# Filling a 0/1 attention mask by row-copying DMAs between SBUF partitions, in a fused attention and FFN kernel

## The chip, the cores and the metric

The kernel runs on one core of a Trainium2 chip. The metric is the device time of one execution, in microseconds (us). The engines are named as in the profile: PE is TensorE (PEld its weight loads), DVE is VectorE, ACT is ScalarE, POOL is GpSimd and SP is SyncE. "PEq", "SPq" and so on are their instruction queues.

## The reference

Block-sparse attention (batch 4, 8 heads, 768 positions, head size 64, blocks of 32) feeds a gated feed-forward network (FFN). Shortened:

```python
scores = q @ k.T / 8
mask = window of +-1 block | first/last block row and column | 3 random blocks per block row
attn = softmax(where(mask, scores, -1e9))
x = (attn @ v), heads side by side           # 3072 x 512
out = (sigmoid(x @ w_gate) * (x @ w_val)) @ w_out   # 512 -> 1536 -> 512, f32
```

The mask has 24 x 24 blocks. It is the same for all batches and heads, and depends on an input (`sampled_blocks`), so the kernel has to make it.

## The kernel before

Keys lie on partitions, queries along the free axis. Partition p of key tile t holds token 6p + t. So partition 16a + i of tile t belongs to block row 3a + (6i + t)//32. The tile `mask` is 128 partitions x 6 key tiles x 768 queries of f16. The 24 block rows, widened to 768 columns, are in `mb24` (24 partitions). A matmul with a 24 x 128 selector spreads them over the partitions, and DVE copies the result from PSUM:

```python
def mask_tile(c0, c1, t):
    n = c1 - c0
    w = 512 // n
    bank = Bank("m")
    def mm(eng):
        for i in range(w):
            nc.tensor.matmul(spare[bank.slot][:, i * n : (i + 1) * n],
                e24[:, (t + i) * 128 : (t + i + 1) * 128], mb24[:, c0:c1],
                start=True, stop=True)
    def evac(eng):
        copy(eng, mask[:, t : t + w, c0:c1],
             spare[bank.slot].rearrange("a (w n) -> a w n", w=w))
    a = plan.add([(PE, 0.25)], mm, t_rows, at=12.0, take=[bank])
    return plan.add([(DVE, 0.69)], evac, [a], free=[bank])
# ...
# Step.mul: exp(scores) times the mask, for all query units but the first
m = mask[:, 2 * self.j : 2 * self.j + 2, self.u * UQ : (self.u + 1) * UQ]
nc.vector.tensor_tensor(self.pt, self.pt,
    m.unsqueeze(1).broadcast_to([128, 2, 2, UQ]), op=ALU.mult)
```

Work is cut into 12 units of 256 queries (4 batches x 3). The first unit adds a bias by matmul and needs no mask; unit 1 is the first to multiply by it. The FFN of unit n runs beside the attention of unit n + 1. `plan.add(engines, fn, deps)` gives tasks with estimated costs to a planner, which fixes each engine's instruction order when the kernel is built. On the chip every engine kept that order, and waited where its next instruction was not ready (in the changed kernel DVE stood for 14.76 us at one instruction, and ran the one behind it, which did not need what was waited for, only then). With a list of two engines the planner takes the one that is free first.

Inputs are f32 and are cast to f16 by the loads, which GpSimd issues. The order is q, k, v of batch 0 in pieces, the first quarter of the FFN weights, the rest of q of batch 0 (the "late q load"), the other FFN weights, and then k, q, v of batch 1. The last three are issued only once the copies of batch 0 have freed the buffers and GpSimd's earlier issues, some of which wait for the landing of older loads (in the kernel before, the issue at 17.48 us after a wait of 1.05 us), are through.

The softmax here doesn't subtract the row's maximum and nothing guards it: scores larger than these inputs give would overflow.

Of the kernel before, what the change touches and what calls it, by code (L numbers as in the profile page):

```python
# [20 lines left out]
B, H, S, D = 4, 8, 768, 64  # L21
BLK = 32
NB = S // BLK
NT = S // 128
# [6 lines left out]
UQ = 256  # L31
NU = S // UQ
PE, ACT, DVE, DMA = "PE", "ACT", "DVE", "DMA"
# [90 lines left out]
def kernel(  # L124
# [11 lines left out]
    nc = tc.nc  # L136
# [34 lines left out]
    e24 = e64[0:NB, :]  # L171
    bias = sing.tile([128, UQ], f16)
    mask = sing.tile([128, NT, S], f16)
# [54 lines left out]
    mb24 = sing.tile([NB, S], f16)  # L228

    def copy(eng, dst, src):  # L230
        if eng == ACT:
            nc.scalar.copy(dst, src)  # L232
        else:
            nc.vector.tensor_copy(dst, src)  # L234
# [22 lines left out]
    plan = Plan({'m': 4, 's': 2})  # L257
    spare = [ps.tile([128, 512], f32, name=f"m{i}") for i in range(4)]
# [5 lines left out]
    def ring(nm, bufs):  # L264

        i = len(used[nm]) - bufs
        return [used[nm][i]] if i >= 0 else []

    def m16(slot):
        return spare[slot].bitcast(f16)  # L270
# [25 lines left out]
    t_rows = []  # L296
    bank = Bank("m")
# [19 lines left out]
    mm = plan.add([(PE, 0.25)], bias_mm, [t_mb], take=[bank])  # L317
    plan.add([(PE, 0.9)], lambda eng: warm(2), [mm])
    t_bias = plan.add([(DVE, 0.35)], bias_out, [mm])
    t_rows.append(plan.add([(DVE, 0.6), (ACT, 0.6)], rows_out, [t_bias], at=12.0, free=[bank]))  # L320

    def more_rows():
        bank = Bank("m")

        def more_mm(eng):
            nc.tensor.matmul(
                spare[bank.slot][0:NB, 0 : S - 512],
                mb16[:, 0:NB],
                e24[:, 512:S],
                start=True,  # L330
                stop=True,
            )

        def more_out(eng):
            copy(eng, mb24[:, 512:S], spare[bank.slot][0:NB, 0 : S - 512])

        mm = plan.add([(PE, 0.15)], more_mm, [t_mb], at=12.0, take=[bank])
        t_rows.append(plan.add([(DVE, 0.35), (ACT, 0.37)], more_out, [mm], free=[bank]))

    def mask_tile(c0, c1, t):  # L340
        n = c1 - c0
        w = 512 // n
        bank = Bank("m")

        def mm(eng):
            for i in range(w):
                nc.tensor.matmul(  # L347
                    spare[bank.slot][:, i * n : (i + 1) * n],
                    e24[:, (t + i) * 128 : (t + i + 1) * 128],
                    mb24[:, c0:c1],  # L350
                    start=True,
                    stop=True,
                )

        def evac(eng):
            copy(
                eng,
                mask[:, t : t + w, c0:c1],
                spare[bank.slot].rearrange("a (w n) -> a w n", w=w),
            )  # L360

        a = plan.add([(PE, 0.25)], mm, t_rows, at=12.0, take=[bank])
        return plan.add([(DVE, 0.69)], evac, [a], free=[bank])

    def prep(src, dst, b, p, t0, t1, deps, at):

        bank = Bank("m")
        box = []

        def pair(eng):  # L370
            pr = work.tile([128, NT, 2, D], f16, tag="pr", bufs=PB, name="pr")
            box.append(pr)
            nc.vector.tensor_copy(  # L373
                pr[:, t0:t1, :, :],
                src[:, 2 * p : 2 * p + 2, t0:t1, :].rearrange(
                    "a h t d -> a t h d"
                ),
            )

        def turn(eng):  # L380
            for t in range(t0, t1):
                nc.tensor.transpose(  # L382
                    m16(bank.slot)[:, (t - t0) * 128 : (t - t0 + 1) * 128],
                    box[0][:, t, :, :],
                    ident,
                )

        def evac(eng):
            copy(
                eng,  # L390
                dst[b % 2][:, p, t0 * 128 : t1 * 128],
                m16(bank.slot)[:, 0 : (t1 - t0) * 128],
            )

        n = t1 - t0
        a = plan.add([(DVE, 0.15 + 0.035 * n)], pair, ring("pr", PB) + loaded[b], at=at)
        copies[b].append(a)
        c = plan.add([(PE, 0.058 * n)], turn, [a], take=[bank])
        used["pr"].append(c)
        return plan.add(  # L400
            [(DVE, 0.14 + 0.07 * n), (ACT, 0.18 + 0.1 * n)], evac, [c] + deps, free=[bank]
        )

    def pair_up(src, dst, b, p, deps, at):
# [77 lines left out]
    class Pair:  # L482
# [72 lines left out]
        def xt(self):  # L555
            if self.n >= 2:
                deps = [used["xT"][self.n - XB]] if self.n >= XB else []
                c = plan.add([(DMA, 0.05)], self.xbar, [self.normed] + deps, lag=6.0)
                used["x16"].append(c)
                xdone[self.n].append(c)  # L560
                return
            c = plan.add([(PE, 0.12)], self.turn, [self.normed], take=[self.bank2])
            used["x16"].append(c)
            deps = [used["xT"][self.n - XB]] if self.n >= XB else []
            xdone[self.n].append(
                plan.add([(DVE, 0.29), (ACT, 0.37)], self.evac, [c] + deps,
                         free=[self.bank2])
            )

# [153 lines left out]
    masks, kdone, qdone, vdone, read, turned_b = {}, {}, {}, {}, {}, {}  # L723
    preps, valued, turned = deque(), deque(), deque()

    def prep_k(b, p, at=0.0):
        kdone[b, p] = [prep(k16, kT, b, p, 0, NT, [], at)]

    def prep_q(b, p, at=0.0, t0=0, t1=NT):
        d_ = [prep(q16, qT, b, p, t0, t1, [], at)]  # L730
        for u in range(t0 // 2, t1 // 2):
            qdone[b, p, u] = d_
# [87 lines left out]
    for p in range(NP):  # L820
        prep_q(0, p, land["q2", None], 2, NT)
    more_rows()
    for t in range(0, NT, 2):
        m = [mask_tile(UQ, S, t + i) for i in range(2)]
        for u in (1, 2):
            masks[t // 2, u] = m
    for j in range(3):
        preps.append(lambda j=j: masks.update({(j, 0): [mask_tile(0, UQ, 2 * j)]}))
    later(1)

    parts = deque()
# [5 lines left out]
    for n in range(1, len(units)):  # L837
        b, u = units[n]
# [63 lines left out]
```

## Time and profile before

| | before |
|---|---|
| time, 3 runs | 298.45 us median (298.33 to 299.55) |
| span of the profiled run | 297.6 us |
| PE busy | 289.9 us (97%) |
| first mask multiply starts | 27.10 us |
| FFN of unit 0 starts on PE | 29.3 us |
| casting loads end (packet records) | about 53 us |

These lines are from the page of the kernel before. The slices cut the span into 40 equal parts of 7.4 us; a digit is the busy share in tenths (PEclk: the granted clock in tenths of full speed; DMA: the mean of 16 engines). GB/s is what the DMA engines moved. Then come the chain of work that ended last, as shares of the span, and one group of instructions: after its count stand the busy time in us and the mean ns of one.

```profile
PE 289.9 (97%) x3302; PEld 206.2 (69%) x3302; DVE 191.0 (64%) x439; ACT 205.1 (69%) x323; POOL 48.5 (16%) x65
...
PE   7998999999999999999999999999999999999994
...
PEclk9999999999999999999999999999999999999999
DMA  7999999999900200999940202920201200201101
GB/s 109 185 201 203 206 204 205 212 174 149 193 12 9 90 13 10 173 177 133 179 70 18 83 11 56 203 64 20 79 11 20 79 11 20 78 15 20 70 2 71
...
PE 92%; ACT 2%; DMA 2%; DVE 1%; POOL 1%; issue 0%; ACTq 0%; POOLq 0%
...
L234 DVE CAST mask<-m 128x512 f16<-128x512 f32 x9 | 5.7, 681 | 0.4 <-PE m L347 0.4
```

PE is the limit. The DMA engines are full from the second slice to the eleventh; up to about 53 us that is the casting loads, at about 200 GB/s. The nine mask copies cost 5.7 us of DVE, and DVE has 36% of the span free.

The chain of the kernel before, around the place where the mask is first used (start us, duration us, what):

```profile
26.14 2.77 ACT pt L469 x3
...
28.95 0.39 PE s L459 x4
29.34 0.98 PE m L617 x8
```

The same stretch in the timeline of the kernel before (start us, duration us, engine, line, operation, tiles, and in brackets the idle time before and what ended it):

```profile
26.61 0.88 POOL L188 DMA_DIRECT2D k<-in_k_dram  x1 [1.45 <-DVE mask L234]
...
27.10 0.69 DVE L475 TENSOR_TENSOR pt<-pt,mask 128x1024 f16<-128x1024 f16 x1 [0.18 <-ACT pt L469]
...
29.28 0.39 PE L617 MATMUL m<-xT,wg 128*128 128x256 f16 x2
```

The first mask multiply starts at 27.10 us, 0.18 us after the DVE instruction before it, and it waited for the exp on ACT, not for the mask. So the mask costs nothing in waiting here. FFN tile 0 (L617) follows at 29.3.

### The profile page before, as it was taken

The numbers are of one execution on the slowest core, as the hardware profiler recorded it, in microseconds if no ns is written. First come the engines' busy times: TensorE is split into PE (matmuls) and PEld (weight loads), VectorE is DVE, ScalarE is ACT, GpSimd is POOL, SyncE is SP. The second block draws the span as 40 slices with busy tenths as digits, with TensorE's granted clock in tenths as the row PEclk, the third lists the DMA queues.
The fourth block names the chain that finished last, engine by engine and source line by source line (L and its number), as shares of the span: only waits on it lengthen the run. The fifth ranks groups of instructions, "written<-read, shape, count | busy, mean of one in ns | idle before, by whom it ended". The sixth has DMA issues, their size and how long they took to land.

```text
span 297.6 us, 7862 instructions
## 1 busy us (share of the span) xinstructions
PE 289.9 (97%) x3302; PEld 206.2 (69%) x3302; DVE 191.0 (64%) x439; ACT 205.1 (69%) x323; POOL 48.5 (16%) x65
## 2 busy tenths in 40 slices
PE   7998999999999999999999999999999999999994
PEld 2655785786786786786776786686687687687771
DVE  3588877875675677676576577577477477475240
ACT  2689977677677677677777776777777677672331
POOL 8944100197000000097100000000000000000000
PEclk9999999999999999999999999999999999999999
DMA  7999999999900200999940202920201200201101
GB/s 109 185 201 203 206 204 205 212 174 149 193 12 9 90 13 10 173 177 133 179 70 18 83 11 56 203 64 20 79 11 20 79 11 20 78 15 20 70 2 71
DMA packets 74540, 28.55 MB, mean 96 GB/s; under 512 B 57352, under 2 KB 71560, under 8 KB 74504
## 3 DMA queue, kind: packets, MB, share of 16 engines
q0 software_dynamic: 40400, 14.16, 43.7%
q1 hardware_dynamic: 33924, 13.75, 20.5%
q8 instruction: 26, 0.43, 0.6%
q10 hardware_dynamic: 180, 0.13, 0.1%
q14 instruction: 10, 0.08, 0.1%
HBM read 28.55 MB, written 6.29 MB: 117 GB/s over the span
## 4 chain that ended last, share of the span: by engine, by line
PE 92%; ACT 2%; DMA 2%; DVE 1%; POOL 1%; issue 0%; ACTq 0%; POOLq 0%
PE m L617 44%; PE m L657 22%; PE s L459 12%; PE m L497 12%; DMA k<-in_k_dram 2%; ACT pt L469 2%; PE s L451 1%; PE m L382 1%; PE m L347 1%; ACT qT L232 0%; PE m L518 0%; POOL k L188 0%; ACT kT L232 0%; POOL q L188 0%; POOL v L188 0%
## 5 line engine op out<-in xcount | busy, mean ns | idle before, releaser
L469 ACT ACTIVATE pt<-s 128x1024 f16<-128x1024 f32 x144 | 139.9, 1023 | 9.5 <-PE s L459 9.4
L475 DVE TENSOR_TENSOR pt<-pt,mask 128x1024 f16<-128x1024 f16 x132 | 91.0, 690 | 52.0 <-ACT pt L469 51.9
L628 ACT ACTIVATE th<-m 128x256 f32<-128x256 f32 x144 | 54.3, 388 | 48.0 <-PE m L617 47.2
L617 PE MATMUL m<-xT,wg 128*128 128x256 f16 x576 | 86.8, 273 | 0.3 <-DVE x L509 0.3
L617 PE MATMUL m<-xT,wv 128*128 128x256 f16 x576 | 86.4, 273 | 0.0
L633 DVE SCALAR_TENSOR_TENSOR ht<-th,m 128x256 f16<-128x256 f32 x144 | 56.6, 417 | 20.8 <-ACT th L628 20.5
L657 PE MATMUL m<-wo,ht 128*128 128x512 f16 x288 | 66.1, 380 | 0.0
L617 PEld LDWEIGHTS <-wv 128*128 128x128 f16 x576 | 56.3, 98 | 6.5
L617 PEld LDWEIGHTS <-wg 128*128 128x128 f16 x576 | 50.5, 98 | 14.8 <-issue 9.7
L657 PEld LDWEIGHTS <-ht 128*128 128x128 f16 x288 | 26.5, 98 | 32.8 <-issue 4.2
L459 PE MATMUL s<-qT,kT 64*128 64x256 f16 x576 | 48.0, 275 | 1.1 <-ACT pt L469 0.8
L497 PEld LDWEIGHTS <-pt 128*128 128x128 f16 x1152 | 43.3, 98 | 3.8 <-issue 0.6
L497 PE MATMUL m<-vex,pt 128*128 128x65 f16 x1152 | 45.1, 194 | 0.0
L459 PEld LDWEIGHTS <-kT 64*128 64x128 f16 x576 | 23.0, 95 | 17.4 <-issue 13.6
L694 ACT ACTIVATE ysb<-m 128x512 f32<-128x512 f32 x23 | 13.7, 597 | 23.7 <-PE m L657 23.7
L740 POOL DMA_DIRECT2D kp<-in_k_dram x16 | 13.0, 820 | 80.8 <-DMA kT<-kp 53.7
L509 DVE TENSOR_TENSOR x<-m,rz 128x256 f16<-128x256 f32 x48 | 20.4, 424 | 1.7
L507 DVE RECIPROCAL rz<-m 128x4 f32<-128x4 f32 x48 | 8.7, 181 | 15.1 <-PE m L497 15.1
L740 POOL DMA_DIRECT2D qp<-in_q_dram x16 | 13.0, 819 | 2.2 <-DMA kp<-in_k_dram 1.9
L451 PE MATMUL s<-bias,e 64*128 64x256 f16 x48 | 7.2, 319 | 0.2 <-ACT pt L469 0.2
L382 PE MATMUL m<-ident,pr 128*128 128x128 f16 x48 | 5.2, 264 | 0.8 <-DVE pr L373 0.4
L234 DVE CAST mask<-m 128x512 f16<-128x512 f32 x9 | 5.7, 681 | 0.4 <-PE m L347 0.4
(45 smaller groups left out, 67.2 us busy)
## 6 DMA issues: line engine op xcount, KB each, us to landing
out_dram<-ysb SPq DMA_DIRECT2D x23, 256.0 KB, 2.0
v<-in_v_dram POOLq DMA_DIRECT2D x3, 768.0 KB, 11.1
wg<-in_moe_w_gate_dram POOLq DMA_DIRECT2D x4, 384.0 KB, 12.8
wv<-in_moe_w_val_dram POOLq DMA_DIRECT2D x4, 384.0 KB, 14.0
wo<-in_moe_w_out_dram POOLq DMA_DIRECT2D x3, 512.0 KB, 16.9
kp<-in_k_dram POOLq DMA_DIRECT2D x16, 96.0 KB, 5.8
qp<-in_q_dram POOLq DMA_DIRECT2D x16, 96.0 KB, 4.9
k<-in_k_dram POOLq DMA_DIRECT2D x4, 192.0 KB, 5.8
```

What stands on the lines that cost most here:

```text
L451: nc.tensor.matmul(score[self.bank.slot][:, o // D, i, :], e64[o : o + D, t * 128 : (t + 1) * 128], bias[o : o + D, :], start=True, stop=F ...
L459: nc.tensor.matmul(score[self.bank.slot][:, o // D, i, :], kT[b % 2][o : o + D, p, t * 128 : (t + 1) * 128], qT[b % 2][o : o + D, p, u * U ...
L469: nc.scalar.activation(self.pt, score[self.bank.slot], AF.Exp, bias=0.0, scale=SCALE)
L475: nc.vector.tensor_tensor(self.pt, self.pt, m.unsqueeze(1).broadcast_to([128, 2, 2, UQ]), op=ALU.mult,)
L497: nc.tensor.matmul(self.acc[:, s, a, :], self.steps[t // 2].pt[:, a, t % 2, s * 128 : (s + 1) * 128], vex[self.b % 2][:, 2 * self.p + a, t ...
L509: nc.vector.tensor_tensor(self.x16, self.acc[:, :, :, 0:D], rz.broadcast_to([128, 2, 2, D]), op=ALU.mult,)
L617: nc.tensor.matmul(pg[:, i, :], w[:, c, f * 128 : (f + 1) * 128], xTs[self.n][0][:, c, :], start=(c == 0), stop=(c == 3),)
L628: nc.scalar.activation(th, spare[bank.slot][:, 0:UQ], AF.Tanh, bias=0.0, scale=0.5)
L633: nc.vector.scalar_tensor_tensor(self.ht[:, f, :], in0=box[0], scalar=1.0, in1=spare[bank.slot][:, UQ : 2 * UQ], op0=ALU.add, op1=ALU.mult,)
L657: nc.tensor.matmul(spare[bank.slot], self.ht[:, f, s * 128 : (s + 1) * 128], wo[:, f, :], start=(f == 0), stop=(f == NF - 1),)
L694: nc.scalar.activation(ysb, spare[bank.slot], AF.Copy, bias=0.0, scale=0.5)
L740: nc.gpsimd.dma_start(dst[:, p, :, a, :], src[b, 2 * p + a].rearrange("(n t) d -> n t d", t=NT),)
```

## The change

The intent is to take the mask off PE and DVE. After `mb24` is ready, 18 DMAs on SP copy its rows to the partitions of `mask`. Each DMA serves 8 partitions, 16 apart, which take 8 different rows, and repeats each row for up to six key tiles: 8 x 6 pieces of 1536 B. In all that is 768 pieces and 1.18 MB. Beside it, the head's copies out of PSUM that ACT could also take are given to DVE alone (except one).

```diff
-    t_rows.append(plan.add([(DVE, 0.6), (ACT, 0.6)], rows_out, [t_bias], at=12.0, free=[bank]))
+    t_rows.append(plan.add([(DVE, 0.6)], rows_out, [t_bias], at=12.0, free=[bank]))
-    def mask_tile(c0, c1, t):           # (body cut)
+    def mask_rows(deps):
+        parts = ((0, 0, 5, 0, 6), (0, 5, 6, 0, 2), (1, 5, 6, 2, 6), (1, 6, 10, 0, 6),
+                 (1, 10, 11, 0, 4), (2, 10, 11, 4, 6), (2, 11, 16, 0, 6))
+        def go(eng):
+            rows = mb24.rearrange("(a c) n -> a c n", c=3)
+            dst = mask.rearrange("(a i) t n -> a i t n", i=16)
+            for c, i0, i1, t0, t1 in parts:
+                for i in range(i0, i1):
+                    nc.sync.dma_start(dst[:, i, t0:t1, :],
+                        rows[:, c, :].unsqueeze(1).broadcast_to([8, t1 - t0, S]))
+        return plan.add([(DMA, 0.05)], go, deps, lag=8.0)
...    # prep(): copies of qT and kT
-            [(DVE, 0.14 + 0.07 * n), (ACT, 0.18 + 0.1 * n)], evac, [c] + deps, free=[bank]
+            [(DVE, ...), (ACT, ...)][: 2 - ((b, p) != (0, 0))], evac, [c] + deps, free=[bank]
...    # copies of xT, units 0 and 1
-                plan.add([(DVE, 0.29), (ACT, 0.37)], self.evac, [c] + deps,
+                plan.add([(DVE, 0.29)], self.evac, [c] + deps,
...    # every mask (j, u) now depends on the one task mask_rows(t_rows)
```

The planner is told `lag=8.0`: it orders the engines as if the mask landed 8 us after its issue. In the order that it then fixes, DVE has the first mask multiply ahead of the last xT copy of unit 0 and of all FFN gating.

More of the change, by code (lines that the diff above doesn't have):

```diff
@@ L338, in more_rows @@
         t_rows.append(plan.add([(DVE, 0.35), (ACT, 0.37)], more_out, [mm], free=[bank]))
-    def mask_tile(c0, c1, t):
-        n = c1 - c0
-        w = 512 // n
-        bank = Bank("m")
-        def mm(eng):
-            for i in range(w):
-                nc.tensor.matmul(
-                    spare[bank.slot][:, i * n : (i + 1) * n],
-                    e24[:, (t + i) * 128 : (t + i + 1) * 128],
-                    mb24[:, c0:c1],
-                    start=True,
-                    stop=True,
-                )
-        def evac(eng):
-            copy(
-                eng,
-                mask[:, t : t + w, c0:c1],
-                spare[bank.slot].rearrange("a (w n) -> a w n", w=w),
-            )
-        a = plan.add([(PE, 0.25)], mm, t_rows, at=12.0, take=[bank])
-        return plan.add([(DVE, 0.69)], evac, [a], free=[bank])
+    def mask_rows(deps):
+        parts = (
+            (0, 0, 5, 0, 6),
+            (0, 5, 6, 0, 2),
+            (1, 5, 6, 2, 6),
+            (1, 6, 10, 0, 6),
+            (1, 10, 11, 0, 4),
+            (2, 10, 11, 4, 6),
+            (2, 11, 16, 0, 6),
+        )
+        def go(eng):
[3 more added lines that the diff above has]
+                for i in range(i0, i1):
+                    nc.sync.dma_start(
+                        dst[:, i, t0:t1, :],
+                        rows[:, c, :]
+                        .unsqueeze(1)
+                        .broadcast_to([8, t1 - t0, S]),
+                    )
+        return plan.add([(DMA, 0.05)], go, deps, lag=8.0)
     def prep(src, dst, b, p, t0, t1, deps, at):
@@ L400, in prep @@
         return plan.add(
-            [(DVE, 0.14 + 0.07 * n), (ACT, 0.18 + 0.1 * n)], evac, [c] + deps, free=[bank]
+            [(DVE, 0.14 + 0.07 * n), (ACT, 0.18 + 0.1 * n)][: 2 - ((b, p) != (0, 0))], evac, [c] + deps, free=[bank]
         )
@@ L822 @@
     more_rows()
-    for t in range(0, NT, 2):
-        m = [mask_tile(UQ, S, t + i) for i in range(2)]
-        for u in (1, 2):
-            masks[t // 2, u] = m
+    rows = [mask_rows(t_rows)]
     for j in range(3):
-        preps.append(lambda j=j: masks.update({(j, 0): [mask_tile(0, UQ, 2 * j)]}))
+        for u in range(NU):
+            masks[j, u] = rows
     later(1)
```

## The prediction

> **What bounds it now.** TensorE: the page gives PE 289.9 of 297.6 us busy (97%), the chain of waits 92% PE. From about 36 us the timeline shows matmuls back to back. Slack exists only before: the chain has ACT pieces at 16.0 (0.80 us), 25.0 (1.10), 26.1 (2.77, exps) and 33.3 (1.03), then DVE until 35.95.
>
> **Removed.** 12 mask matmuls: 1.5 us of PE chain (1.9% of its first 80 us). Nine mask copies on DVE, 5.7 us busy. Moved from ACT to DVE: the 24x512 row copy (0.56), one kT copy (0.80), two qT copies (0.58 each), late xT copies (0.37 each): about 3.5 us of ACT where ACT is in the chain. Alone this is worth 2 to 3.5 us.
>
> **Added.** 18 DMAs on the SP queue, 768 row pieces of 1536 B, 1.18 MB. As built, the first VectorE mask multiply waits for nearly all of them; behind it stand the last xT copy and all FFN gating, so TensorE must stop before FFN tile 0 (29.3 us now). The first DMA can go when the second row copy ends, about 16.8 us.
>
> The slices show the DMA engines at 9 of 9 and about 205 GB/s from 10 to 53 us: the casting loads. [...]here 8, so 96 pieces each. [...]at 77 to 79 us, beside a load, about 7 store packets per 0.1 us started over 16 engines, and 16 load packets: one store packet per engine each 0.23 us. For the smaller 1536 B pieces (65 ns each in the e64 load) I estimate 0.12 to 0.2 us, so 11 to 19 us for 96. With 1.4 us of start-up the mask lands at 29 to 38 us, middle 33.5.
>
> The loads lose that time on the same engines: the late q load, landed at about 22.3 us, comes 2 to 4 us later, and with it unit 1's scores, so FFN tile 0 starts no earlier than about 31 us. Later loads mostly still make their use.
>
> **Sum.** FFN tile 0 starts at mask + 1.1 us (multiply, xT copy), about 34.6, 5.3 later than now. One score step more is left by then, +0.4; the ACT gap at 33 to 36 us is filled, -1.5; a long stall may return the PE clock to its slow start rate (0.21 instead of 0.11 us per matmul before 14 us), +0.5. That makes 303; weighing a quicker mask, 302 us, range 296 to 309. Faster by over 2%: 0.04; within: 0.61; slower: 0.35.
>
> **What would show it.** Mask issues from about 17 us; the first multiply waiting on DMA, at 29 to 38 us instead of 27.1; TensorE idle just before FFN tile 0; the chain through mask DMAs; then dense matmuls, same tail. ACT busy lower by 3.5 us, DVE by 3.
>
> **What would make it wrong.** If the pieces spread over 16 engines[...], the mask lands by 26 us: a gain of 2 to 3 us. If [...]issue is slow (over 0.8 us per DMA), it lands after 40 us: 309 or more.

Marked cuts take out the general grounds that were given for two figures, and two cases that rested on them; no trace of this case shows them as rules. No term of the sum is cut. The mask: issue at 16.8 us, 1.4 of start-up and 15.3 for 96 pieces (the middle of 11 to 19) make 33.5. The time: 5.3 us by which FFN tile 0 is later, + 0.4 - 1.5 + 0.5, make 4.7 us more than before, 303 us, weighed down to 302. "Here 8" is the number of DMA engines to one mask DMA: it was an assumption then, and the records of the changed kernel, below, agree with it (eight landing increments for each). The 1.4 us is an estimate for which no source was given: in the kernel before, SP's stores had their first packet 0.83 to 0.84 us after the start of the issue where the queue was quiet. That a stall may slow the PE clock was a guess as well; the rates beside it, 0.21 and 0.11 us, are of the kernel before, and the clock after the stall was measured below.

## The result, and the profile after

The changed kernel takes 313.64 us (median of 4 runs, 313.1 to 314.1) against 298.89 (median of 4 on the same chip). The ratio is 1.0492, 95% interval 1.0459 to 1.0524. Ratios are the mean time of one kernel's fast runs over that of the other's of the same rounds, so they are not quite the ratio of the medians quoted. The prediction of 302 us (296 to 309) was too low.

| | before | after |
|---|---|---|
| span of the profiled run | 297.6 | 311.6 |
| mean granted PE clock | 0.998 | 0.973 |
| mask usable | not waited for | 40.9 us |
| first mask multiply | 27.10 | 41.17 |
| FFN tile 0, as in the chain | 29.34 | 42.12 |
| from there to the end | 268.3 | 269.5 |

The page after, the lines that answer to those above. Slices are of 7.8 us. The last line is a group of DMA issues (count, KB each) and stands in the place of the mask copies, which are gone:

```profile
PE 286.9 (92%) x3290; PEld 204.6 (66%) x3290; DVE 188.3 (60%) x438; ACT 202.1 (65%) x315; POOL 48.6 (16%) x65
...
PE   6874059999999999999999999999999999999995
...
PEclk9799559999999999999999999999999999999999
DMA  7999999669993020089992020193110110110101
GB/s 114 181 210 193 194 201 193 103 138 189 133 182 71 19 73 16 17 154 178 144 214 19 8 86 12 41 175 92 44 53 8 44 53 8 44 54 18 69 0 67
...
PE 85%; DMA 9%; DVE 2%; POOL 1%; issue 1%; ACT 0%; DVEq 0%; SPq 0%; POOLq 0%
...
mask<-mb SPq DMA_DIRECT2D x14, 72.0 KB
```

PE is idle in the fifth slice (31 to 39 us), and its clock is halved there and in the next. In the eighth slice (55 to 62 us) the DMA engines move only 103 GB/s; what this is, the packet records below show. The chain of waits after, where it passes through the mask:

```profile
17.86 0.14 SPq L358
...
18.04 6.37 DMA mask<-mb
...
24.43 8.09 DMA mask<-mb
...
32.53 8.33 DMA mask<-mb
...
41.17 0.13 DVE pt L477
...
41.78 0.30 DVE xT L234
...
42.12 1.23 PE m L619 x5
```

Three DMA flights in a row make up the stall. At most eight of the 18 DMAs are out at a time: in the program as built, the ninth waits for the landing of the first, the seventeenth for the ninth. So three flights of 6.4, 8.1 and 8.3 us follow one another. Then the multiply, the xT copy behind it in DVE's order, and FFN tile 0. The timeline after shows the same from the side of DVE and PE:

```profile
41.17 0.69 DVE L477 TENSOR_TENSOR pt<-pt,mask 128x1024 f16<-128x1024 f16 x1 [14.76 <-DMA mask<-mb]
...
41.78 0.28 DVE L234 COPY xT<-m 128x256 f16<-128x256 f16 x1
...
42.12 0.37 PE L619 MATMUL m<-xT,wg 128*128 128x256 f16 x1 [14.23 <-DVE xT L234]
```

DVE waited 14.76 us for the mask, and PE 14.23 us for an xT copy that does not need the mask at all but stands behind the multiply.

The shift of FFN tile 0, 42.12 - 29.34 = 12.8 us, is most of the loss. Is the work behind it the same? The windows from FFN tile 0 to the end say so. The columns are the window's length, then busy us (and count) of PE, PEld, DVE, ACT and POOL, the granted clock, the DMA share and GB/s. Before:

```profile
29.34:297.60 268.26, 264.12 (x3013) 191.14 (x3012) 171.51 (x384) 185.38 (x300) 29.03 (x36) 1.00 0.59 87
```

After:

```profile
42.12:311.60 269.48, 265.77 (x3013) 191.13 (x3012) 172.79 (x388) 184.03 (x296) 28.12 (x35) 0.99 0.55 82
```

The same 3013 matmuls took 1.65 us more of PE time, and the idle time among them fell from 4.1 to 3.7 us (length less busy time). Five-microsecond windows of the kernel after show where the slow matmuls are:

```profile
30.00:35.00 5.00, 0.00 (x0) 0.00 (x0) 0.00 (x0) 0.00 (x0) 0.88 (x1) 0.66 1.39 194
35.00:40.00 5.00, 0.00 (x0) 0.00 (x0) 0.00 (x0) 0.00 (x0) 0.87 (x1) 0.50 1.34 189
40.00:45.00 5.00, 2.88 (x15) 1.54 (x15) 2.69 (x5) 1.01 (x2) 0.87 (x1) 0.50 1.31 203
45.00:50.00 5.00, 5.00 (x70) 3.20 (x69) 3.89 (x9) 3.99 (x8) 0.00 (x0) 0.97 1.28 205
```

From 30 to 40 us PE, DVE and ACT do nothing, while the DMA engines move 190 GB/s. The clock records of the trace have it at half from 31.7 to 45.3 us. PE has been idle since 27.9 us when the clock falls 3.8 us later, and it is full again 3.2 us after PE restarts at 42.12.

The trace also records every DMA packet: start, queue, size, duration. Counted in stretches of 3 us, they are not a view of the page but a sum over the records:

```
stretch us   before: loads KB/us   after: loads KB/us   after: mask KB/us (pieces)
24 to 27            199                  130                  63  (123)
30 to 33            201                  130                  63  (123)
45 to 48            199                  202                   0
54 to 57              0                  109                   0
57 to 60              0                  102                   0
```

While the mask pieces run, the total is as before (193 against 200 KB/us), so every mask byte is taken from the loads. After the loads of before are over, those of after go on at half rate until 64.7 us. That is what is left if eight of the 16 engines fell behind and the other eight are done. The semaphore records of the trace fit: after one increment at its issue, each mask DMA lands by eight more, and of the 16 with which k of batch 1 lands, eight came at 45.4 to 47.6 us and eight at 55.5 to 57.3 (in the kernel before, all between 43.7 and 45.6). From the eight increments and the half rate I take it that each mask DMA used eight engines. (Experiment 5 has DMAs of the same shape alone on the engines: there the mean busy share of the 16 was three to four tenths.) I work out an estimate from the table and these eight: if the eight engines without mask pieces kept their half of 200 KB/us, the other eight carried about 30 KB/us of loads, or about 118 load packets of 768 B in 3 us beside 123 mask pieces. So there is about one load packet to each mask piece. And 123 pieces on eight engines in 3 us is one per engine each 0.195 us.

The first piece starts at 21.4 us, 4.2 us after the first issue at 17.2. The last starts at 39.6.

### The profile page after: what moved, and what is told of

Its sections match the earlier page's. It is cut to its first block, busy times and chain, and to the rows that moved or that the text cites. A ratio compares the mean times of both kernels' runs of the same rounds, so it can differ in the third digit from the quotient of the medians.

```text
span 311.6 us, 7854 instructions
## 1 busy us (share of the span) xinstructions
PE 286.9 (92%) x3290; PEld 204.6 (66%) x3290; DVE 188.3 (60%) x438; ACT 202.1 (65%) x315; POOL 48.6 (16%) x65
## 4 chain that ended last, share of the span: by engine, by line
PE 85%; DMA 9%; DVE 2%; POOL 1%; issue 1%; ACT 0%; DVEq 0%; SPq 0%; POOLq 0%
PE m L619 42%; PE m L659 21%; PE s L461 11%; PE m L499 11%; DMA mask<-mb 7%; DMA k<-in_k_dram 2%; POOL k L188 0%; POOL q L188 0%; POOL v L188 0%; DVE kT L234 0%; DVE vex L430 0%; DVE mb L234 0%; DVE pr L375 0%; PE m L384 0%; PE m L520 0%
## 5 line engine op out<-in xcount | busy, mean ns | idle before, releaser
L619 PEld LDWEIGHTS <-wv 128*128 128x128 f16 x576 | 56.7, 98 | 21.3 <-issue 14.4
L384 PE MATMUL m<-ident,pr 128*128 128x128 f16 x48 | 4.1, 235 | 3.6 <-DVE pr L375 3.6
L453 PE MATMUL s<-bias,e 64*128 64x256 f16 x48 | 6.5, 296 | 0.3 <-ACT pt L471 0.3
L384 PEld LDWEIGHTS <-pr 128*128 128x128 f16 x48 | 3.0, 104 | 5.2 <-DVE pr L375 5.0
```

The lines of the kernel that those rows point to most:

```text
L619: nc.tensor.matmul(pg[:, i, :], w[:, c, f * 128 : (f + 1) * 128], xTs[self.n][0][:, c, :], start=(c == 0), stop=(c == 3),)
```

## The experiments

The main theory: the mask lands late because its 768 pieces share eight DMA engines with the casting loads, and the DVE multiply waits for it with the xT copy behind. The rivals, taken up in turn: the head copies moved from ACT to DVE; the added traffic by itself, without any wait; a fixed time per piece, whatever its size; the partitions that a DMA writes or reads; and the DMAs' issue on SP.

### 1. The head copies alone

The kernel before, with only the moves from ACT to DVE:

```diff
-[(DVE, 0.6), (ACT, 0.6)], rows_out
+[(DVE, 0.6)], rows_out
 # and the same for the copies of kT and qT (but one) and of xT
```

> The mask stays with matmuls and copies as before; only the head copies are moved to VectorE. Theory (the loss is the wait for the mask DMAs): 297.5 to 300 us, ratio 0.997 to 1.006, because TensorE is dense from 36 us on and the moved copies only trade ACT slack for VectorE work in a stretch where VectorE still has 5.7 us of mask copies. Rival (the moved copies delay VectorE and make part of the 15 us): over 302 us.

Measured: 300.62 us (299.44 to 301.08), ratio 1.0065, interval 1.0042 to 1.0089. This is about 2 us of loss and just outside the top of the range expected. It is not the cause of 15 us, but the prediction's "alone this is worth 2 to 3.5 us" does not hold: the moves gave nothing by themselves. I have not tested why they cost 0.65%. That stays open.

### 2. The DMAs alone

The changed kernel with the head copies put back as before.

```diff
-[(DVE, 0.6)], rows_out
+[(DVE, 0.6), (ACT, 0.6)], rows_out
 # and the same for kT, qT and xT
```

> The mask comes by the 18 DMAs; the head copies may go to ACT as before. Theory (the mask DMAs are the whole loss): the last mask DMA lands at 40 to 41 us as in the changed kernel, and the time is 311 to 315 us. Rival (copies on VectorE hold up the rows that feed the DMAs and are part of the loss): 310 us or less.

Measured: 314.27 us (313.37 to 315.05), ratio 1.0528, interval 1.0504 to 1.0552. DVE waited 14.4 us for the mask, as its waits between 14 and 75 us show (total us, times, longest):

```profile
DVE pt L477 <- DMA mask<-mb: 14.4, 1, 14.4
```

All of the loss comes with the DMAs.

### 3. The traffic without the wait

The kernel before, with its matmul-made mask and its order on PE, DVE and ACT, and in addition the 18 DMAs into a tile that nobody reads:

```diff
+    mask2 = sing.tile([128, NT, S], f16, name="mask2")
+    # mask_rows as in the change, but dst = mask2.rearrange(...)
+    mask_rows(t_rows)
     for t in range(0, NT, 2):
         m = [mask_tile(UQ, S, t + i) for i in range(2)]
```

> Kernel before with the same compute order, plus the 18 mask DMAs into a tile that nobody reads. It separates the cost of the traffic from the cost of the wait. Theory: the loads lose engine time on the eight engines that the mask uses and end at about 63 us instead of 53; the batch 1 k load, used at 47.0 us, lands at 52 to 57, so VectorE stops at the kp copies and the kernel takes 301 to 307 us. Rival (only the wait costs): 298.3 to 299.5 us.

Measured: 309.37 us (308.72 to 309.58), ratio 1.0361, interval 1.0343 to 1.038. This is well above the range expected, and the theory as I held it (that nearly everything is the mask wait) falls. Without one instruction waiting for the mask DMAs, they cost 10.8 us. The chain of this kernel shows through what:

```profile
32.80 23.99 DMA k<-in_k_dram
56.81 1.17 DVE kp L436 x4
57.98 0.34 DVE ht L661
```

And its waits between 14 and 75 us (engine, line, what it waited for: total us, times, longest):

```profile
DVE kp L436 <- DMA k<-in_k_dram: 8.1, 1, 8.1
...
PEld L685 <- DVE ht L661: 5.1, 1, 5.1
```

k of batch 1 was issued at 32.80, not at 26.61. (The trace puts GpSimd's wait before it down to a DVE instruction that ended at 32.55. In the changed kernel the same issue comes at 32.59, after a wait of 4.66 us that is put down to the landing of a weight load. I take the late loads for the cause in both, but no run separates the two.) It then shared the engines with what was left of the others, and landed at 56.8 (45.6 in the kernel before). DVE stands still for it at the `kp` copies, which repack k, and with it the FFN gating (`ht`) that PE needs. The granted clock was halved in the eighth slice, at 54 to 62 us.

### 4. Half the bytes

Key tiles 2j and 2j + 1 of one partition always lie in the same block row, so half a mask is enough. This is the changed kernel with 18 DMAs that repeat each row up to three times in place of six:

```diff
-    mask = sing.tile([128, NT, S], f16)
+    mask = sing.tile([128, NT // 2, S], f16)
-            (0, 0, 5, 0, 6), ...
+            (0, 0, 5, 0, 3), ...
-            m = mask[:, 2 * self.j : 2 * self.j + 2, ...]      # broadcast over heads
+            m = mask[:, self.j, ...]                           # and over the two key tiles
```

> As the changed kernel with 18 DMAs, but each brings one mask row per pair of key tiles (both tiles of a pair have the same row), so half the pieces and bytes: 48 pieces of 1536 B on each engine. Theory (the time goes per piece on the busy engines, 0.19 us each): pieces take about 9 us from 21 us on, the mask lands at 30 to 32.5 us, time 301 to 304.5 us. Rival (the time goes per DMA: three rounds of at most eight in flight, about 8 us a round whatever their size): lands at 38 to 41, 311 to 314 us.

Measured: 306.81 us (306.16 to 307.53), ratio 1.028, interval 1.0259 to 1.03. The mask was there at 33.3 us, a little over the range expected and far from the 38 to 41 of the rival. The time was above the range expected. Bytes or pieces on the engines thus matter, but no longer all of it. In the packet records its pieces, of the same 1536 B and beside the same loads, took 78 ns in the median; in the changed kernel it is 140. The chain now shows issue slots one after another (seven of them in a row, one shown):

```profile
18.39 5.22 DMA mask<-mb
...
24.26 0.60 SPq L358
...
28.14 5.14 DMA mask<-mb
...
34.55 1.23 PE m L619 x5
...
38.67 1.43 PE m L499 x24
```

With small DMAs the limit has moved to SP, 0.6 us for each, plus 5.2 us of flight at either end. The last line is the halved clock again: 24 value matmuls took 1.43 us against 0.77 later. From 34.55 to 40.10 the chain takes 5.55 us. At the rates of the changed kernel after 47 us (0.98 for eight FFN matmuls, 0.33 for four score and 0.77 for 24 value matmuls) I estimate 3.0 us for the same.

### 5. The same DMAs on quiet engines

The changed kernel with copies of `mb24` appended after its last store, when nothing else moves. The weight tiles are overwritten then, which does no harm. Its time says nothing.

```diff
     plan.run()
+    for parts, step in ((8, 16), (8, 4), (16, 8)):
+        for i in range(9):      # nine DMAs: 8 partitions 16 apart; 8, 4 apart; 16, 8 apart
+            nc.sync.dma_start(dst[:, i % 3, :, :],
+                src.unsqueeze(1).broadcast_to([parts, NT, S]))
```

> The changed kernel, with 27 more mask copies appended after all work, when no load is in flight, into tiles no longer needed: first 9 DMAs exactly like those of the mask (8 destination partitions 16 apart), then 9 with 8 partitions 4 apart, then 9 with 16 partitions 8 apart. It measures the disputed cost alone. Theory (the pieces of 1536 B are slow, 125 to 150 ns, only because they run beside the casting loads): alone every group shows 65 to 85 ns, and the first piece starts within 1.5 us of the issue[...]. Rival (eight partitions 16 apart [...]are slow by themselves): group one shows 110 ns or more, group two 65 to 85. Issue on SP 0.6 us each in any case. The total is about 15 to 20 us longer than the changed kernel and means nothing.

The first line of the added DMAs in SP's timeline (three issues to a line):

```profile
309.71 1.96 SPq L884 DMA_DIRECT2D wg<-mb  x3
```

Measured, from the packet records: the first piece started 1.3 us after the start of the issue and 0.6 us after its end (4.2 and 3.4 in the changed kernel, beside the loads). The median piece took 68 ns with destinations 16 apart and 71 with 4 apart, and in both groups a quarter of the pieces took about 125 or more. So on quiet engines it makes no difference whether the destinations lie 16 or 4 apart; beside loads this was not tested. Nine DMAs needed 6.0 us and were paced by the issues, 0.65 us each as the line shows. The third group, with 16 partitions, surprised me. The DMA share, the mean of 16 engines, was three to four tenths in nearly all of the slices before it and eight to nine in it, so about twice as many were busy. Yet its median piece took 233 ns and a DMA 1.5 us: about 96 GB/s against about 105 before it, no better rate. I do not know why. This group also reads 16 neighbouring partitions in place of eight that lie three apart, and no run separates the two. As it stands, the obvious repair of spreading each DMA wider is not shown to help.

### 6. The columns of unit 1 first

The changed kernel with three sets of 18 DMAs, 512 B pieces, ordered by the unit that needs them:

```diff
-    def mask_rows(deps):
+    def mask_rows(deps, u):         # only columns u * UQ : (u + 1) * UQ
...
+    for u in (1, 2, 0):
+        rows = [mask_rows(t_rows, u)]
```

> As the changed kernel, but the mask comes in three sets of 18 DMAs, first the 256 columns that unit 1 needs, then unit 2's, then unit 0's; pieces of 512 B instead of 1536, as many per set as before in all. Theory by bytes (a piece is slow because of its bytes): unit 1's set is bound by the issue of about 0.65 us per DMA and the start under load, lands at 33 to 35 us, FFN tile 0 starts at 34 to 36; the loads are still late, the time is 305 to 310 us. Rival (each piece costs [...]0.19 us whatever its bytes): unit 1's set lands at 39 to 42 and the time is 311 us or more.

Measured: 306.14 us (305.69 to 308.95), ratio 1.0256, interval 1.0216 to 1.0295. The first multiply started at 31.7 us, earlier than expected, after a wait of 4.2 us (waits between 10 and 40 us):

```profile
DVE pt L477 <- DMA mask<-mb: 4.2, 1, 4.2
```

The number of pieces before it was the same 768 as in the change, each a third the size, with a median of 40 ns. If a piece cost a fixed 0.19 us, the wait would have ended at 39 to 42 us. So that rival falls: here the landing went with the bytes and the issues.

### 7. Half the mask, made by matmuls

The tile pairs of experiment 4 in the kernel before: six mask matmuls in place of 12, with fewer copies. It is a candidate to beat both.

```diff
-                    e24[:, (t + i) * 128 : (t + i + 1) * 128],
+                    e24[:, 2 * (t + i) * 128 : (2 * (t + i) + 1) * 128],
 # and the mask tile and multiply of experiment 4
```

> The kernel before, with the mask still made by matmuls and copies but one row per pair of key tiles: 6 mask matmuls instead of 12, and 3 copies of 512 columns, one of 2x256 and one of 256 instead of nine of 512. Theory: about 0.75 us less on TensorE before 26 us, 2.6 us less on VectorE where it is partly in the chain: ratio 0.994 to 0.999, faster by 0.3 to 1.8 us. Rival (that stretch is bound by ACT and by the q load): no difference, 0.999 to 1.002.

Measured in 5 rounds: 298.80 us (297.6 to 300.89), ratio 0.9993, interval 0.996 to 1.0026. The FFN began at 27.07 us in the profiled run, 2.3 us before its time in the kernel before, yet the timed runs show no gain at the end. The profiled run is the fastest of its six: its span, 295.8 us, is 1.8 us below the 297.6 of the kernel before, so it kept most of that lead, and the other runs can't be looked into.

### 8. The DMAs issued early

The changed kernel with the rows copied at about 5 us and the DMAs issued from 5.84 us, so that they cannot be late:

```diff
-rows_out, [t_bias], at=12.0, free=[bank])
+rows_out, [t_bias], free=[bank])
+    more_rows()
+    rows = [mask_rows(t_rows)]          # ahead of the first unit's work
     prs = [Pair(0, p) for p in range(NP)]
```

> As the changed kernel, but the rows are copied at about 5 us and the mask DMAs issue from about 6 us, so that they would be there in time. Theory (the traffic itself costs, because the loads are needed just in time): the mask lands at 26 to 31 us and no longer stops VectorE for more than 3 us, but the first k, q and v loads come 2 to 5 us later on the mask's engines and the batch 1 k load still lands at 54 to 58, so the time is 305 to 312 us. Rival (only the late start of the mask costs): 300 us or less.

Measured: 308.21 us (308.0 to 308.8), ratio 1.0309, interval 1.0281 to 1.0337. No wait for the mask is left. In the waits of this kernel between 4 and 42 us another stands in its place, and the chain leads through it:

```profile
DVE pr L375 <- DMA q<-in_q_dram: 8.0, 3, 4.9
```

The late q load landed at 32.3 us, about 10 us later than in the kernel before, and FFN tile 0 started at 38.70. Moved forward, the mask took its bytes from the loads that the first unit needs.

### 9. Other source partitions

In the change, one DMA reads eight rows three partitions apart. Here they are four apart, on 32 partitions, which changes where in SBUF they are read:

```diff
-    mb24 = sing.tile([NB, S], f16)
+    mb24 = sing.tile([32, S], f16)      # rows made at partitions 4a + c
-            rows = mb24.rearrange("(a c) n -> a c n", c=3)
+            rows = mb24.rearrange("(a c) n -> a c n", c=4)
```

> As the changed kernel with the same 18 DMAs, pieces and destinations; only the rows that the DMAs read are laid out four partitions apart per group (row 3a+c in partition 4a+c) instead of three[...]. Theory[...]: pieces of 78 to 100 ns instead of 140, the mask lands at 33 to 36 us instead of 40.9, the time is 305 to 309 us. Rival (the pieces are slow because of the loads' own traffic, whatever the source): lands at 40 to 42, 312 to 315 us.

Measured: 314.07 us (313.4 to 314.57), ratio 1.0505, interval 1.0481 to 1.0529. The first multiply started at 41.27 us, and the median piece took 136 ns (140 in the changed kernel). The wait for the mask is still there:

```profile
DVE pt L483 <- DMA mask<-mb: 15.6, 1, 15.6
```

My theory that the place of the source rows alone slows the pieces falls. The destinations still lie 16 apart here, and no run moves both.

### 10. The traffic, with its consumers later

Experiment 3 again, with the copies of k, q and v of batch 1 planned 11 us later in DVE's order, so that nothing stands still for a late load:

```diff
-pair_up(src, dst, b, p, loaded[b], land[nm, "next"])
+pair_up(src, dst, b, p, loaded[b], land[nm, "next"] + 11)
 # and the same for v
```

> As traffic_only, but the kp, qp and v copies of batch 1 stand about 11 us later in VectorE's order (the order is fixed at build), so a late load stops nobody unless unit 3's scores need it. Theory (traffic costs only because the k load is late at the kp copies, 8.1 us of VectorE wait): that wait is gone or under 2 us, the time is 299 to 304 us; a part may come back where unit 3 waits for its transposed keys. Rival (the traffic costs through something else): 307 us or more.

Measured: 304.45 us (303.65 to 304.99), ratio 1.0183, interval 1.0159 to 1.0207. That is just above the range expected. The wait for k is gone, and with it 309.37 - 304.45 = 4.9 us, about half of what the traffic costs. Of the rest, 3.45 us are already there at FFN tile 0. It starts at 32.79, and the chain shows the late q load, landed at 25.7 us, in front of it:

```profile
11.45 14.22 DMA q<-in_q_dram
25.70 0.30 DVE pr L401
```

### 11. Experiment 7 with its consumers later

In experiment 7 the order is planned earlier while the loads land when they did. If its early gain was lost in a wait for k, copies 4 us later should give it back:

```diff
-pair_up(src, dst, b, p, loaded[b], land[nm, "next"])
+pair_up(src, dst, b, p, loaded[b], land[nm, "next"] + 4)
```

> As half_matmul, with the kp, qp and v copies of batch 1 about 4 us later in VectorE's order. half_matmul reached FFN tile 0 about 2.3 us earlier than the kernel before in its profiled run and yet was no faster in the timed runs. Theory (in the timed runs it then waits for the k load, which is just in time): ratio 0.990 to 0.996, 295.5 to 297.5 us. Rival (the early gain is lost elsewhere): 0.997 to 1.002.

Measured in 5 rounds: 300.34 us (298.78 to 302.23), ratio 1.0044, interval 1.0009 to 1.0079. The theory falls. Where the 2.3 us went stays open.

### 12. The loads held back

The changed kernel with the same order on PE and DVE. GpSimd now issues the later weight loads, and all loads behind them, only when the mask has landed:

```diff
-    for j in range(1, NF // FCH):       # at the start of the kernel
-        load_w(j)
-    for j in range(3):
-        load_wo(j)
+        def held(eng):                  # after mask_rows
+            nc.gpsimd.tensor_copy(seen, mask[:, :, 0:1])
+            # ... the same loads here; the loads of batch 1 wait for this task too
```

> The changed kernel with its compute order unchanged on TensorE and VectorE; GpSimd holds back every load from the second weight group on until the mask has landed, so that the 18 mask DMAs have the engines to themselves once the q load (about 22 us) is in. Theory (beside loads the DMAs are slow; alone they are bound by the issue on SP, 0.65 us each, as the appended copies were): the mask lands at 30 to 33 us instead of 40.9 and FFN tile 0 starts at 31 to 34. What was won comes back later, because the held loads are then 10 us or more late: total 306 to 318 us. Rival (the mask DMAs are slow by themselves in this place, loads or not): lands at 38 us or later.

Measured: 312.13 us (311.38 to 313.31), ratio 1.0454, interval 1.0423 to 1.0485. The mask landed at 30.96 us, 15.1 us after the first issue at 15.87; in the changed kernel it took 23.7. Its chain shows issue slots and two flights (eight of 0.6 us in a row, one shown):

```profile
16.70 5.97 DMA mask<-mb
...
27.16 0.60 SPq L356
...
27.80 3.15 DMA mask<-mb
```

So 8.6 of the 23.7 us are contention with the loads that were held back. The other 15 us are SP's issues and two flights, the first of them still beside the late q load (its packets start until 22.3 us), and would be late as well: 31 us is after the 27.1 at which the mask is wanted. Between 23 and 30 us no load ran beside the mask, and yet its median piece took 118 ns. So the loads alone do not make the pieces slow. Its waits between 14 and 75 us show where the cost came back:

```profile
DVE pt L486 <- DMA mask<-mb: 4.6, 1, 4.6
...
DVE kp L419 <- DMA k<-in_k_dram: 5.6, 1, 5.6
```

The loads held back are late for their own use, as in experiment 3.

### All together

| kernel | time, us | ratio | mask or first multiply, us |
|---|---|---|---|
| before | 298.45 | 1 | 27.10 (no wait) |
| the change | 313.64 | 1.0492 | 40.9 |
| 1 head copies alone | 300.62 | 1.0065 | no mask DMAs |
| 2 DMAs alone | 314.27 | 1.0528 | DVE waits 14.4 |
| 3 traffic without wait | 309.37 | 1.0361 | no wait for it |
| 4 half the bytes | 306.81 | 1.028 | 33.3 |
| 6 unit 1 first | 306.14 | 1.0256 | 31.7 |
| 7 half, by matmuls | 298.80 | 0.9993 | no mask DMAs |
| 8 issued early | 308.21 | 1.0309 | no wait for it |
| 9 other sources | 314.07 | 1.0505 | 41.27 |
| 10 traffic, late consumers | 304.45 | 1.0183 | no wait for it |
| 11 half, late consumers | 300.34 | 1.0044 | no mask DMAs |
| 12 loads held back | 312.13 | 1.0454 | 30.96 |

The nearest version with mask DMAs (10) is 1.8% slower than the kernel before, and none of the others is shown to beat it.

## Why the prediction was right or wrong

**Right: the mechanism.** The prediction named the mask DMAs in SP's queue beside the casting loads, eight engines, the first multiply waiting with the last xT copy and the gating behind it, TensorE idle before FFN tile 0, and the chain through the mask DMAs. All of it is in the profile after, and experiment 2 shows that it comes with the DMAs. The busy times moved as said: ACT 205.1 to 202.1 (-3.0 against -3.5), DVE 191.0 to 188.3 (-2.7 against -3). Multiply and xT copy after the landing took 1.2 us against 1.1.

**Wrong: "the mask lands at 29 to 38 us, middle 33.5".** This is the step that failed. The mask landed at 40.9, 7.4 us after that middle. The terms, predicted and measured:

| term | predicted | measured |
|---|---|---|
| first issue | 16.8 us | 17.2 |
| issue to first piece | 1.4 us | 4.2 |
| 96 pieces on each engine | 15.3 us (0.16 each) | 18.2 (0.19 each) |
| last piece's start to mask usable | none | 1.3 |
| sum | 33.5 | 40.9 |

The start-up was estimated without regard to the loads. Experiment 5 measured 1.3 us on a quiet queue, but beside the loads it is 4.2. The start-up and the 96 pieces were each almost 3 us too short. Evidence lay in the trace of the kernel before and was overlooked: a store issued at 73.69 us, beside a load, had its first packet at 77.2. The time per piece was inside the range given (0.12 to 0.2), but near its top. The last term was left out. The prediction does say that a mask after 40 us means 309 us or more, but the reason that it gives for that did not hold: an issue took 0.6 us, not over 0.8.

**Wrong: "weighing a quicker mask, 302".** The sum was 303. The tilt of -1 went towards a quicker mask, for which the prediction names the spreading over 16 engines. That did not happen: each mask DMA landed by eight increments, and the mask was late.

**Wrong in size: the terms after FFN tile 0.** The prediction added 0.4 (score step) - 1.5 (ACT gap) + 0.5 (clock), -0.6 in all; measured was +1.2. The ACT pieces did leave the chain there. But the same 3013 matmuls took 1.65 us more, with the clock at half from the stall to 45.3 us. In the chain, 42.12 to 45.57 takes 3.45 us for 13 FFN and four score matmuls at the half clock. At the later rates (0.98 for eight, 0.33 for four) I estimate 1.9 us for them; the other 1.5 us are nearly all of that difference.

**Right in the changed kernel, wrong as a statement about the traffic: "Later loads mostly still make their use".** In the changed kernel k of batch 1 is issued 6 us later too (32.59 against 26.61), but the mask stall has pushed its users back by more: k landed at 57.3 and was first copied at 63.2. Experiment 3 shows what is hidden there: the traffic alone costs 10.8 us. The costs overlap, and do not add. Experiments 4, 6, 8 and 12 each took one of them away, and the time was still at least 2.5% above the kernel before. In 8 and 12 it was seen that another load then arrived late. The expected delay of the late q load by 2 to 4 us did not occur in the changed kernel's profile (landed at 22.9 against 22.2 us, after an issue 0.8 us later), since the first piece came only at 21.4. It does show in experiments 8 and 10, where the DMAs start earlier.

**Wrong: the gain of the moved copies.** "Alone this is worth 2 to 3.5 us" covered both the removed matmuls and the moved copies. Experiment 1 shows no gain from the copies (+0.65%). Experiment 7 takes away six mask matmuls and shows no gain either. The room in the head is not simply convertible to time at the end.

**What stays open.** What sets the time of a mask piece. It is not simply the loads: the median piece took 140 ns in the changed kernel, 78 in experiment 4 beside the same loads, and 118 in experiment 12 where no load ran. Experiments 5 and 9 changed destinations and sources one at a time, so an effect of both together is not excluded. Why the copies on DVE cost 0.65%. Where experiment 7's 2.3 us went.

## What to carry to other kernels

The DMAs that replaced compute were not free here, where the DMA engines were full (9 tenths busy in the kernel before, up to 53 us with the casting loads): while the mask moved 63 KB/us, the loads fell from 199 to 130. So look first at the DMA share of the stretch where the new transfer will run. If it is full as it was here, count each byte of the transfer as taken from the loads beside it, and ask which consumer of those loads will wait, even if the new transfer itself is not waited for (in experiment 3 the copies of k did, for 8.1 us). Take start-up and time per piece from transfers in the trace that run beside the same load (the start-up was 4.2 us here, and 1.3 on quiet engines), and add the issue time on the queue (0.6 us for each small DMA here, 11 us for the 18). Where the order of an engine is fixed, look at what stands behind the first instruction that waits for the new transfer: here DVE waited 14.76 us there, and an xT copy behind it, which did not need the mask, kept PE idle for 14.23 us. PE then restarted at half clock, for 3.2 us.
